# A long convolution by real transforms with a gated output: second stage with 128 moving columns, columns put right in the last table

## The chip, the cores and the metric

The kernel runs on one core of a Trainium2 chip. The metric is device time in microseconds, as the median of several runs. PE is the matrix engine (its weight loads are listed as PEld), DVE the vector engine, ACT the scalar engine, POOL the general engine, and SP the engine whose queue issues all DMA here. Matmuls write to PSUM, which DVE and ACT read and POOL doesn't.

## The reference

For x of shape [8, 6400, 128] and h of shape [6400, 128] (sequence, channel), the reference makes a causal convolution along the sequence, per channel, and then a gated mix of the channels, all in float32:

```python
Xf = np.fft.rfft(x, n=2*S, axis=1); Hf = np.fft.rfft(h, n=2*S, axis=0)
y = np.fft.irfft(Xf * Hf[None], n=2*S, axis=1)[:, :S]        # _attn_ref
for k in range(5):                                            # _moe_ref, on y
    gate_pre += conv_w[k] * y_padded[:, k:k + S]              # 4 zeros ahead
gate = 1 / (1 + np.exp(-gate_pre))
out = (gate * (y @ w_val)) @ w_out
```

## The kernel before, in words

**The transform.** The sequence is split as 6400 = N1 x N2 = 100 x 64, and the convolution is done by four stages of small matmuls with cosine and sine tables instead of an FFT. One frequency index is k1 (100 values, in two halves of HR = 50), the other k2 (64 values).

- *First stage* (`Forward`): a load brings XG = 4 channel pairs as XR = 114 rows (two channels, 50 rows each, the first padded to 64). POOL forms the difference and DVE or POOL the sum of mirrored halves (`sums`), and 16 matmuls, which the chip runs as 32 instructions since each float32 matmul is two, multiply them with the table r1 (`half`). ACT (and DVE in the opening) copies PSUM to `gh` for h or `gy` for a batch.
- *Second stage* (`s2_mm`, L271): for each block kb of SB = 4 values of k1 within a half (13 blocks, the last with 2), each value has its own table in m2. 128 rows are contracted to 64; output goes to the lower or the upper 64 PSUM partitions. Each matmul moves 64 columns: half of the channels. Four matmuls per value and component (two halves p of k1 times two channel halves k) go to the output half (p + k) % 2, so that the other half of the channels has the k1 halves exchanged.
- *Product* (`Product`, L302): with the spectrum of h, which was made in the same layout by `Spectrum`. DVE multiplies PSUM with the first component into `gy` (`mul_u`) and with the second into one of three tiles `w_t` (`mul_t`); POOL adds and subtracts (`add`). The spectrum of h is kept in DRAM (`hd`) and loaded again, block by block, for each later batch (`h_load`).
- *Third stage* (`s3_quads`): contracts the 64 values of k2, four 64 x 64 matmuls abreast, 128 columns each; ACT and DVE copy to `dt`.
- *Last stage* (`Chunk.s4`, L371): for each of the 64 positions n2, four matmuls with 100 columns of the table m4 (`m4v`, L345) give y, in 13 chunks of five positions (the head chunk: four).

**The gate.** Per chunk ACT copies y and makes some of the five taps straight from PSUM, DVE makes others, POOL adds one (`copies`, `taps`); then come PE's projection, ACT's sigmoid, DVE's product, PE's output matmul, and a copy and store.

**Order.** All instructions keep program order on their engines, written out by hand.

- *The opening*: the first stage for h, then for batch 0. The load ring has the three `x_sb` tiles and twelve more that lie in the not yet loaded m4 table.
- *The head*: the second stage for h (13 `Spectrum`) and batch 0 (13 `Product`) in turn. DVE decodes the 64-bit weights between products (`weights`). Each spectrum block is stored to `hd`.
- Then, per batch b, *stage A*: 16 groups, each with the third stage of batch b and the first of batch b + 1, the m2 and h loads for what follows, and a step of the `trail`, the late chunks of the batch before (`Gates.trail`); in batch 0 also 13 loads of m4. And *stage B*: 13 steps, each with the last stage of a chunk of batch b and the second stage and product of block s + 1 of batch b + 1; project, output and store of earlier chunks follow two to four steps behind. Chunks at DEFER = 40 or later (40, 45, 50, 55) only copy y in B; their taps, projection, gate, output and store, and those of the head chunk, are the trail of the next A. The last batch has no trail: it finishes in order.
- SP issues loads and stores in program order: in B, per step, an m load (after the block that used its tile), a store, and an h load (after the second DVE product, L632). Rings: m2 has M2B = 4 tiles, h has HB = 3, `w_t` has WB = 3.
- PSUM: two pools of two bank pairs in the opening and the head; afterwards one of them makes way for four single banks, which the third and last stage, projection and output share.

Of the kernel before, what the change touches and what calls it, by code (L numbers as in the profile page):

```python
# [10 lines left out]
F32 = mybir.dt.float32  # L11
# [21 lines left out]
NCH = len(CHUNKS)  # L33
OUT_ORDER = CHUNKS[1:] + [HEAD]
LATE = 35
DEFER = 40
M2B = 4
WB = 3
HB = 3
XB = 3  # L40


def _out_range(ch):
# [8 lines left out]
def _constants():  # L52
    k1 = np.arange(N1, dtype=np.float64)
    n1 = np.arange(N1, dtype=np.float64)
    k2 = np.arange(N2, dtype=np.float64)
    n2 = np.arange(N2, dtype=np.float64)
    half = np.arange(2 * HP) % HP
    own = half < HR
    tau = 2.0 * np.pi
    a = tau * np.outer(half + 0.5, k1 + 0.25) / N1  # L60
    r1 = np.stack([np.cos(a) + np.sin(a), np.cos(a) - np.sin(a)], axis=1) * own[:, None, None]
    al = tau * (
        (k1[None, :, None] + 0.25) * n2[:, None, None] / N
        + np.outer(n2, k2)[:, None, :] / N2
        - (k1[None, :, None] + 0.25) / (2 * N1)
    )
    co, si = np.cos(al) / 2, np.sin(al) / 2
    m2 = np.zeros((2, N2, N1, 2 * N2))
    m2[0, :, :, :N2] = co - si
    m2[0, :, :, N2:] = -si - co  # L70
    m2[1, :, :, :N2] = co + si
    m2[1, :, :, N2:] = co - si
    m2 = m2.reshape(2 * N2, 2, HR, 2 * N2).transpose(0, 2, 1, 3)
    b = tau * np.outer(k2, n2) / N2
    r3 = np.zeros((N2, 2, N2, 2))
    r3[:, 0, :, 0] = np.cos(b)
    r3[:, 1, :, 0] = -np.sin(b)
    r3[:, 0, :, 1] = -np.sin(b)
    r3[:, 1, :, 1] = -np.cos(b)
    r3 = np.concatenate([r3, r3], axis=0)  # L80
    t = N2 * n1[None, :] + n2[:, None]
    kk = half + HR * (np.arange(2 * HP) // HP)
    g = tau * (kk[:, None, None] + 0.25) * t[None] / N
    m4 = np.concatenate([np.cos(g), np.sin(g[:, :1])], axis=1) / N * own[:, None, None]
    f = lambda v: np.ascontiguousarray(v.astype(np.float32))
    return f(r1.reshape(2 * HP, -1)), f(m2), f(r3.reshape(2 * HP, -1)), f(m4.reshape(2 * HP, -1))

# [22 lines left out]
def longconv_moe(ctx: ExitStack, tc: tile.TileContext, x, h, r1, m2, r3, m4, w64, out):  # L110
# [11 lines left out]
    dt = cp.tile([128, N2 * 2 * C], F32, name="dt")  # L122
    dv = dt.rearrange("p (n c d) -> p n c d", c=2, d=C)
    gh = dt[:, : N1 * C].rearrange("p (d k t) -> p d k t", k=N1, t=2)
    m4_sb = cp.tile([128, N2 + 1, N1], F32, name="m4_sb")
    r1_sb = cp.tile([128, 2, N1], F32, name="r1_sb")
    r3_sb = cp.tile([128, 2, 2 * N2], F32, name="r3_sb")
    w_sb = cp.tile([C, NW], F32, name="w_sb")
# [7 lines left out]
    w_t = [cp.tile([128, 2 * SB * C], F32, name=f"w_{i}") for i in range(WB)]  # L136
# [73 lines left out]
    class Forward:  # L210


        def __init__(self, src, dst, xs=x_sb, o=0):
            self.src, self.dst, self.n, self.s, self.i, self.o = src, dst, 0, 0, 0, o
            self.xs = xs[o % len(xs) :] + xs[: o % len(xs)]

        def load(self, n=1):
            for _ in range(n):
                if self.n < NS:
                    nc.sync.dma_start(self.xs[self.n % len(self.xs)][:XR], self.src[self.n, :XR])  # L220
                    self.n += 1

        def sums(self, e):
            j = self.s
            if j >= NS:
                return
            self.s += 1
            x, sd = self.xs[j % len(self.xs)][:XR], sd_sb[(j + self.o) % 3][:XR]
            nc.gpsimd.tensor_tensor(out=sd[:, 1], in0=x[:, 0], in1=x[:, 1], op=ALU.subtract)
            e.tensor_tensor(out=sd[:, 0], in0=x[:, 0], in1=x[:, 1], op=ADD)  # L230
            self.load()
# [22 lines left out]
    def count(kb):  # L254
        return min(SB, HR - kb * SB)

    def m2_load(kb):
        if kb < NKB:
            n = count(kb)
            nc.sync.dma_start(m2_sb[kb % M2B][:, :n], m2[:, kb * SB : kb * SB + n])  # L260

    def h_load(kb):
        if kb < NKB:
# [4 lines left out]
        n = count(kb)  # L268
        return t[:, : 2 * n * C].rearrange("p (c d k t) -> p c d k t", c=2, k=n, t=2)

    def s2_mm(src, kb):  # L271
        pt = pair()
        n = count(kb)
        v = pt[:, :, : n * C].rearrange("p c (d k t) -> p c d k t", k=n, t=2)
        for s in range(n):
            for c in range(2):
                for p, k in ((0, 0), (1, 0), (1, 1), (0, 1)):
                    o = (p + k) % 2
                    nc.tensor.matmul(
                        v[o * N2 : (o + 1) * N2, c, k * C // 4 : (k + 1) * C // 4, s, :],  # L280
                        lhsT=m2_sb[kb % M2B][:, s, p, c * N2 : (c + 1) * N2],
                        rhs=src[:, k * C // 4 : (k + 1) * C // 4, p * HR + kb * SB + s, :],
                        start=True,
                        stop=True,
                    )
        return v

    hx = h_sb + [dt[:, N1 * C + i * 2 * SB * C : N1 * C + (i + 1) * 2 * SB * C] for i in range(3)]

    class Spectrum:  # L290
        def __init__(self, kb):
            self.kb, self.v = kb, s2_mm(gh, kb)
            self.h = hx[kb % len(hx)]

        def copy(self):
# [4 lines left out]
            nc.sync.dma_start(hd[self.kb, :, :n], self.h[:, :n])  # L300

    class Product:  # L302
        def __init__(self, kb, h=None):
            self.kb, self.v = kb, s2_mm(gy, kb)
            self.t = laid(w_t[kb % WB], kb)
            self.u = gy.rearrange("p d (c k) t -> p c d k t", c=2)[:, :, :, kb * SB : kb * SB + count(kb)]
            self.h = laid(h if h is not None else h_sb[kb % HB], kb)

        def both(self, c):
            h = self.h[:, c : c + 1]  # L310
# [31 lines left out]
            for k in range(2)  # L342
        ]

    def m4v(n, c):  # L345
        if c and n:
            return m4_sb[:, N2 - n, :][:, ::-1]
        return m4_sb[:, N2 if c else n, :]

    def cells(x, n):  # L350

# [10 lines left out]
    class Chunk:  # L362
# [8 lines left out]
        def s4(self):  # L371
            a, n = self.ch
            pt = single()
            for q in range(n):
                for c in range(2):
                    for k in range(2):
                        o = slice(k * HP, (k + 1) * HP)
                        nc.tensor.matmul(
                            pt[o, q * N1 : (q + 1) * N1],
                            lhsT=dv[:, a + q, c, o],  # L380
                            rhs=m4v(a + q, c),
                            start=c == 0,
                            stop=c == 1,
                        )
            self.p = pt[:, : n * N1].rearrange("p (n t) -> p n t", n=n)
# [85 lines left out]
        def store(self):  # L471
# [5 lines left out]

    wgen = weights()
    xh = x_sb + [
        m4_sb.rearrange("p n t -> p (n t)")[:, i * 2 * XG * N2 : (i + 1) * 2 * XG * N2].rearrange(  # L480
            "p (a d n) -> p a d n", a=2, n=N2
        )
        for i in range(12)
    ]
    fh, fx = Forward(h, gh, xh), Forward(x[0], gy, xh, NS)
    fh.load()
# [5 lines left out]
    for g, (f, i) in enumerate(order):  # L492
        e = f.half()
        if g + 2 < 2 * NS:
            order[g + 2][0].sums(nc.vector)
        if g + len(xh) >= NS:
            fx.load()
        e[0](act)
        e[1](act if g % 2 else dve)
    next(wgen)  # L500
    for kb in range(M2B):
        m2_load(kb)
    nc.sync.dma_start(r3_sb, r3)
    sp, pr = {0: Spectrum(0)}, {}
    for kb in range(-1, NKB + 1):
        if 0 <= kb < NKB:
            pr[kb] = Product(kb, sp[kb].h)
            m2_load(kb + M2B)
        if kb + 2 < NKB:
            sp[kb + 2] = Spectrum(kb + 2)  # L510
        if kb + 1 < NKB:
            sp[kb + 1].copy()
            sp[kb + 1].store()
        if 0 <= kb < NKB:
            pr[kb].mul_u()
# [8 lines left out]
    class Gates:  # L524
# [5 lines left out]
        def trail(self):  # L530

            h, late = self.cs[0], [c for c in self.cs if c.late]
            steps = collections.defaultdict(list)
            for m, c in enumerate(late):
                t = 2 * m + m // 2
                steps[t + 4].append(c.store)
                steps[t + 3].append(c.output)
                steps[t + 2] += [c.project, c.sigm, c.gate]
                steps[t].append(lambda c=c: c.taps(range(2)))
                steps[t + 1].append(lambda c=c: c.taps(range(2, 4)))  # L540
            n = max(steps) + 1
# [27 lines left out]
    for b in range(B):  # L569
# [8 lines left out]
        for g in range(NS):  # L578
# [107 lines left out]
```

## Time and profile before

| | us |
|---|---|
| median of 3 runs (lowest to highest) | 1040.47 (1040.33 to 1044.34) |
| the profiled execution's own time | 1044.37 |
| its span, first to last instruction | 1042.5 |
| PE busy in the span | 966.9 |
| DVE, POOL, ACT busy | 687.5, 552.1, 479.9 |

The span is the one core's. Every engine's instructions are recorded on one helper line (L97), so groups are told apart by their tiles: `pt` is PSUM, `r_sb` the tables r1 and r3, `m` the second stage's table, `m_sb` the last table, `h`, `w` and `dt` the spectrum, the second product, and the big tile that holds gh in the opening and head and the third stage's result later. A row of the order of time gives start, duration, engine, line, operation, tiles, shape and count, and in brackets the idle time ahead of it with what ended it. A matmul's duration contains the way through the array; the pace is read from start to start.

### The profile page before, as it was taken

The numbers are of one execution on the slowest core, as the hardware profiler recorded it, in microseconds if no ns is written. First come the engines' busy times: TensorE is split into PE (matmuls) and PEld (weight loads), VectorE is DVE, ScalarE is ACT, GpSimd is POOL, SyncE is SP. The second block draws the span as 40 slices with busy tenths as digits, with TensorE's granted clock in tenths as the row PEclk, the third lists the DMA queues.
The fourth block names the chain that finished last, engine by engine and source line by source line (L and its number), as shares of the span: only waits on it lengthen the run. The fifth ranks groups of instructions, "written<-read, shape, count | busy, mean of one in ns | idle before, by whom it ended". The sixth has DMA issues, their size and how long they took to land.

```text
span 1042.5 us, 54128 instructions
## 1 busy us (share of the span) xinstructions
PE 966.9 (93%) x24960; PEld 809.8 (78%) x24960; DVE 687.5 (66%) x932; ACT 479.9 (46%) x923; POOL 552.1 (53%) x558
## 2 busy tenths in 40 slices
PE   7997777999989998899989999999989999999987
PEld 6897767878787877888788878878788878877753
DVE  3447711897549772896559772996459772996476
ACT  3431133454534455355534455345534465344465
POOL 4534732577427862577437852677427852671032
PEclk9999899999999999999999999999999999999999
DMA  3566465674548554674558554774558554761012
GB/s 140 179 190 200 166 189 178 205 211 135 179 148 235 154 166 144 208 208 141 163 182 232 144 167 132 229 199 142 165 158 235 145 167 135 244 184 43 31 41 88
DMA packets 93409, 171.99 MB, mean 165 GB/s; under 512 B 41952, under 2 KB 50016, under 8 KB 93184
## 3 DMA queue, kind: packets, MB, share of 16 engines
q1 hardware_dynamic: 93184, 168.55, 53.4%
q8 instruction: 196, 3.21, 1.3%
q14 instruction: 29, 0.24, 0.1%
HBM read 135.75 MB, written 32.77 MB: 162 GB/s over the span
## 4 chain that ended last, share of the span: by engine, by line
PE 84%; issue 5%; DMA 4%; DVE 3%; SPq 1%; POOL 1%; ACT 0%; POOLq 0%; DVEq 0%
PE pt L97 84%; DMA x<-xl 1%; DVE gl L97 1%; DMA m_sb<-hl 1%; SPq L97 1%; DMA m_sb<-xl 1%; DVE dt L97 1%; POOL gl L97 1%; POOL dt L97 0%; DVE gy L97 0%; DMA x<-hl 0%; ACT dt L97 0%; DVE w L97 0%; POOLq L682 0%; POOL sd L97 0%
## 5 line engine op out<-in xcount | busy, mean ns | idle before, releaser
L97 POOL TENSOR_TENSOR gy<-gy,w 128x512 f32<-128x512 f32 (+1 forms) x206 | 253.3, 1253 | 85.2 <-DVE w L97 84.5
L97 PEld LDWEIGHTS pt<-r_sb,gy 64*64 64x64 f32 (+1 forms) x8192 | 236.0, 131 | 69.8 <-issue 51.3
L97 PE MATMUL pt<-r_sb,gy 64*50 64x128 f32 (+1 forms) x8192 | 266.6, 275 | 19.2 <-issue 13.0
L97 POOL TENSOR_TENSOR sd<-x 114x256 f32<-114x256 f32 x232 | 189.3, 839 | 162.6 <-issue 102.3
L97 ACT COPY dt<-pt 128x512 f32<-128x512 f32 (+3 forms) x270 | 157.1, 585 | 210.4 <-PE pt L97 205.8
L97 PEld LDWEIGHTS pt<-gy,m 128*64 128x64 f32 x6400 | 204.4, 136 | 40.5 <-issue 22.0
L97 PE MATMUL pt<-gy,m 128*64 128x64 f32 x6400 | 209.2, 221 | 14.8 <-issue 9.3
L97 PEld LDWEIGHTS pt<-m_sb,dt 128*64 128x64 f32 x4096 | 188.7, 137 | 43.6 <-issue 29.1
L97 PE MATMUL pt<-m_sb,dt 128*64 128x100 f32 x4096 | 196.5, 249 | 3.6 <-DVE dt L97 2.4
L97 DVE COPY dt<-pt 128x512 f32<-128x512 f32 (+1 forms) x136 | 92.7, 682 | 149.2 <-PE pt L97 148.2
L97 PE MATMUL pt<-r_sb,sd 50*64 50x100 f32 x4608 | 162.9, 278 | 24.2 <-issue 16.9
L97 PEld LDWEIGHTS pt<-r_sb,sd 50*64 50x64 f32 x4608 | 140.8, 154 | 37.9 <-issue 25.0
L97 DVE TENSOR_TENSOR gy<-pt,h 128x1024 f32<-128x1024 f32 (+1 forms) x98 | 115.2, 1175 | 43.3 <-PE pt L97 43.3
L97 DVE SCALAR_TENSOR_TENSOR dt<-pt,w_sb,dt 128x500 f32<-128x500 f32 (+7 forms) x216 | 132.9, 632 | 14.1 <-POOL dt L97 5.5
L97 ACT COPY gy<-pt 128x400 f32<-128x400 f32 x248 | 110.7, 497 | 60.4 <-PE pt L97 51.0
L97 DVE SCALAR_TENSOR_TENSOR gl<-yl,w_sb,gl 128x500 f32<-128x500 f32 (+1 forms) x119 | 105.5, 892 | 40.9 <-ACT gl L97 38.9
L97 ACT ACTIVATE dt<-pt,w_sb 128x500 f32<-128x500 f32 (+1 forms) x64 | 40.1, 627 | 167.3 <-PE pt L97 161.7
L97 PE MATMUL pt<-dt,w_sb 128*64 128x500 f32 (+2 forms) x480 | 114.8, 555 | 1.9 <-ACT p L97 1.0
L97 DVE TENSOR_TENSOR w<-pt,h 128x1024 f32<-128x1024 f32 (+1 forms) x98 | 114.9, 1172 | 0.0
L97 POOL TENSOR_TENSOR dt<-dt,p 128x500 f32<-128x500 f32 (+1 forms) x64 | 66.5, 1039 | 82.5 <-DVE dt L97 66.5
L97 ACT COPY yl<-pt 128x500 f32<-128x500 f32 (+1 forms) x96 | 54.5, 568 | 66.6 <-PE pt L97 66.6
L97 DVE TENSOR_TENSOR gl<-pt,gl 128x500 f32<-128x500 f32 (+1 forms) x48 | 31.7, 661 | 54.2 <-ACT gl L97 35.5
(34 smaller groups left out, 539.4 us busy)
## 6 DMA issues: line engine op xcount, KB each, us to landing
m<-m SPq DMA_DIRECT2D x96, 512.0 KB
h<-hd SPq DMA_DIRECT2D x84, 512.0 KB
x<-xl SPq DMA_DIRECT2D x116, 228.0 KB
out<-dt SPq DMA_DIRECT2D x56, 250.0 KB
out<-yl SPq DMA_DIRECT2D x40, 250.0 KB
m_sb<-m SPq DMA_DIRECT2D x13, 250.0 KB
hd<-h SPq DMA_DIRECT2D x6, 512.0 KB
hd<-dt SPq DMA_DIRECT2D x6, 512.0 KB
```

The costliest lines, as they stand in the source:

```text
L97: return self._tc.keep_in_program_order(call(*args, **kwargs))
```

## The change

The second stage drops the split of the channels: one matmul per value, component and half p of k1 moves all 128 columns, and half p always goes to output half p. For one half of the channels the two k1 halves are thereby exchanged against the layout of before. What that changes in the third and last stage goes into tables: r3 has its own lower and upper rows (k2 + 1/2 in the upper ones), and the last table now has, for each position, three blocks of 50 columns: those of even n1, those of odd n1, and the odd ones with the sign turned (MW = 150 columns instead of 100). The last stage reads two of the three blocks, the first and second for the one half of the channels and the first and third for the other, and writes them to every other place of PSUM, so that the result has its old order.

The second product is written over the spectrum tile instead of `w_t`, which is gone (in the head, where the spectrum still has to be stored, it goes to three tiles `t_head` within the m4 table). The rings change: h has 4 tiles, m2 has 3, and 6 in the head (three of them in the m4 table). The loads of the first stage bring all 128 rows instead of 114, the opening's ring has 8 tiles instead of 15. DEFER becomes 35, so the chunk at 35 joins the trail, whose steps are placed anew.

```diff
-XR = HP + HR
+MW = 3 * HR
-DEFER = 40
-M2B = 4
-WB = 3
-HB = 3
+DEFER = 35
+M2B = 3
+MH = 6
+HB = 4
 XB = 3
+XH = 8
...
-    b = tau * np.outer(k2, n2) / N2
-    r3 = np.zeros((N2, 2, N2, 2))
...
-    r3 = np.concatenate([r3, r3], axis=0)
-    t = N2 * n1[None, :] + n2[:, None]
-    kk = half + HR * (np.arange(2 * HP) // HP)
-    g = tau * (kk[:, None, None] + 0.25) * t[None] / N
-    m4 = np.concatenate([np.cos(g), np.sin(g[:, :1])], axis=1) / N * own[:, None, None]
+    r3 = []
+    for p in range(2):
+        b = tau * np.outer(k2 + p / 2, n2) / N2
+        c, d = np.cos(b), np.sin(b)
+        g = 1 - 2 * p
+        r3.append(np.stack([np.stack([c, -g * d], -1), np.stack([-d, -g * c], -1)], 1))
+    r3 = np.concatenate(r3, axis=0)
+    t = N2 * n1[None, :] + np.arange(N2 + 1)[:, None]
+    sign = np.where(np.arange(2 * HP)[:, None] < HP, 1.0, 1 - 2 * (n1 % 2))
+    m4 = np.cos(tau * (half[:, None, None] + 0.25) * t[None] / N) / N * own[:, None, None] * sign[:, None]
+    m4 = np.concatenate([m4[:, :, ::2], m4[:, :, 1::2], -m4[:, :, 1::2]], axis=2)
...
-                    nc.sync.dma_start(self.xs[self.n % len(self.xs)][:XR], self.src[self.n, :XR])
+                    nc.sync.dma_start(self.xs[self.n % len(self.xs)], self.src[self.n])
...
-            x, sd = self.xs[j % len(self.xs)][:XR], sd_sb[(j + self.o) % 3][:XR]
+            x, sd = self.xs[j % len(self.xs)], sd_sb[(j + self.o) % 3]
...
+    m4_flat = m4_sb.rearrange("p n t -> p (n t)")
+    m2_head = m2_sb + [
+        m4_flat[:, i * 2 * SB * C : (i + 1) * 2 * SB * C].rearrange("p (s a c) -> p s a c", a=2, c=C)
+        for i in range(M2B, MH)
+    ]
...
-                for p, k in ((0, 0), (1, 0), (1, 1), (0, 1)):
-                    o = (p + k) % 2
+                for p in range(2):
                     nc.tensor.matmul(
-                        v[o * N2 : (o + 1) * N2, c, k * C // 4 : (k + 1) * C // 4, s, :],
-                        lhsT=m2_sb[kb % M2B][:, s, p, c * N2 : (c + 1) * N2],
-                        rhs=src[:, k * C // 4 : (k + 1) * C // 4, p * HR + kb * SB + s, :],
+                        v[p * N2 : (p + 1) * N2, c, :, s, :],
+                        lhsT=ms[kb % len(ms)][:, s, p, c * N2 : (c + 1) * N2],
+                        rhs=src[:, :, p * HR + kb * SB + s, :],
...
+    t_head = [m4_flat[:, i * 2 * SB * C : (i + 1) * 2 * SB * C] for i in range(MH, MH + 3)]
...
-        def __init__(self, kb, h=None):
-            self.kb, self.v = kb, s2_mm(gy, kb)
-            self.t = laid(w_t[kb % WB], kb)
+        def __init__(self, kb, h=None, t=None, ms=m2_sb):
+            self.kb, self.v = kb, s2_mm(gy, kb, ms)
+            h = h if h is not None else h_sb[kb % HB]
...
-            self.h = laid(h if h is not None else h_sb[kb % HB], kb)
+            self.h, self.t = laid(h, kb), laid(t if t is not None else h, kb)
...
-    def m4v(n, c):
-        if c and n:
-            return m4_sb[:, N2 - n, :][:, ::-1]
-        return m4_sb[:, N2 if c else n, :]
+    def m4v(n, c, k):
+        v = m4_sb[:, N2 - n if c else n, :].rearrange("p (b m) -> p b m", m=HR)
+        if c:
+            return v[:, 1::-1, ::-1] if not k else v[:, ::-2, ::-1]
+        return v[:, 0:2, :] if not k else v[:, ::2, :]
...
-                            pt[o, q * N1 : (q + 1) * N1],
+                            pt[o, q * N1 : (q + 1) * N1].rearrange("p (m b) -> p b m", b=2),
                             lhsT=dv[:, a + q, c, o],
-                            rhs=m4v(a + q, c),
+                            rhs=m4v(a + q, c, k),
...
-        if g + len(xh) >= NS:
+        if NS - len(xh) <= g < NS:
             fx.load()
...
-    for kb in range(M2B):
-        m2_load(kb)
+    for kb in range(MH):
+        m2_load(kb, m2_head)
...
-            pr[kb] = Product(kb, sp[kb].h)
-            m2_load(kb + M2B)
+            pr[kb] = Product(kb, sp[kb].h, t_head[kb % 3], m2_head)
+            m2_load(kb + MH, m2_head)
...
-            for m, c in enumerate(late):
-                t = 2 * m + m // 2
-                steps[t + 4].append(c.store)
-                steps[t + 3].append(c.output)
-                steps[t + 2] += [c.project, c.sigm, c.gate]
-                steps[t].append(lambda c=c: c.taps(range(2)))
-                steps[t + 1].append(lambda c=c: c.taps(range(2, 4)))
-            n = max(steps) + 1
-            steps[n - 2] += [h.project, h.sigm, h.gate]
-            steps[n - 1].append(h.output)
-            steps[n].append(h.store)
+            for m, c in enumerate(late + [h]):
+                t = 2 * m + 2
+                if c is not h:
+                    steps[t - 2].append(lambda c=c: c.taps(range(2)))
+                    steps[t - 1].append(lambda c=c: c.taps(range(2, 4)))
+                steps[t] += [c.project, c.sigm, c.gate]
+                steps[t + 2].append(c.output)
+                steps[t + 3].append(c.store)
+            n = max(steps)
```

More of the change, by code (lines that the diff above doesn't have):

```diff
@@ L73, in _constants @@
     m2 = m2.reshape(2 * N2, 2, HR, 2 * N2).transpose(0, 2, 1, 3)
-    b = tau * np.outer(k2, n2) / N2
-    r3 = np.zeros((N2, 2, N2, 2))
[L76 to L79, printed above, removed]
-    r3 = np.concatenate([r3, r3], axis=0)
-    t = N2 * n1[None, :] + n2[:, None]
-    kk = half + HR * (np.arange(2 * HP) // HP)
-    g = tau * (kk[:, None, None] + 0.25) * t[None] / N
-    m4 = np.concatenate([np.cos(g), np.sin(g[:, :1])], axis=1) / N * own[:, None, None]
+    r3 = []
[9 more added lines that the diff above has]
+    m4 = np.concatenate([m4[:, :, ::2], m4[:, :, 1::2], -m4[:, :, 1::2]], axis=2)
     f = lambda v: np.ascontiguousarray(v.astype(np.float32))
@@ L124, in longconv_moe @@
     gh = dt[:, : N1 * C].rearrange("p (d k t) -> p d k t", k=N1, t=2)
-    m4_sb = cp.tile([128, N2 + 1, N1], F32, name="m4_sb")
+    m4_sb = cp.tile([128, N2 + 1, MW], F32, name="m4_sb")
     r1_sb = cp.tile([128, 2, N1], F32, name="r1_sb")
@@ L135, in longconv_moe @@
     sd_sb = [cp.tile([128, 2, XG, N2], F32, name=f"sd_{i}") for i in range(3)]
-    w_t = [cp.tile([128, 2 * SB * C], F32, name=f"w_{i}") for i in range(WB)]
     p_t = [cp.tile([128, CH, N1], F32, name=f"p_{i}") for i in range(2)]
@@ L255, in count, with m2_load @@
         return min(SB, HR - kb * SB)
-    def m2_load(kb):
+    m4_flat = m4_sb.rearrange("p n t -> p (n t)")
[3 more added lines that the diff above has]
+    ]
+    def m2_load(kb, ms=m2_sb):
         if kb < NKB:
             n = count(kb)
-            nc.sync.dma_start(m2_sb[kb % M2B][:, :n], m2[:, kb * SB : kb * SB + n])
+            nc.sync.dma_start(ms[kb % len(ms)][:, :n], m2[:, kb * SB : kb * SB + n])
     def h_load(kb):
@@ L269, in laid, with s2_mm @@
         return t[:, : 2 * n * C].rearrange("p (c d k t) -> p c d k t", c=2, k=n, t=2)
-    def s2_mm(src, kb):
+    def s2_mm(src, kb, ms=m2_sb):
         pt = pair()
@@ L288, in longconv_moe @@
     hx = h_sb + [dt[:, N1 * C + i * 2 * SB * C : N1 * C + (i + 1) * 2 * SB * C] for i in range(3)]
+    t_head = [m4_flat[:, i * 2 * SB * C : (i + 1) * 2 * SB * C] for i in range(MH, MH + 3)]
     class Spectrum:
         def __init__(self, kb):
-            self.kb, self.v = kb, s2_mm(gh, kb)
+            self.kb, self.v = kb, s2_mm(gh, kb, m2_head)
             self.h = hx[kb % len(hx)]
@@ L479, in longconv_moe @@
     xh = x_sb + [
-        m4_sb.rearrange("p n t -> p (n t)")[:, i * 2 * XG * N2 : (i + 1) * 2 * XG * N2].rearrange(
+        m4_flat[:, i * 2 * XG * N2 : (i + 1) * 2 * XG * N2].rearrange(
             "p (a d n) -> p a d n", a=2, n=N2
         )
-        for i in range(12)
+        for i in range(XH - XB)
     ]
@@ L589, in longconv_moe @@
                 a = CH * g
-                nc.sync.dma_start(m4_sb[:, a : a + CH], m4.rearrange("k (n t) -> k n t", t=N1)[:, a : a + CH])
+                nc.sync.dma_start(m4_sb[:, a : a + CH], m4.rearrange("k (n t) -> k n t", t=MW)[:, a : a + CH])
             if nxt and g % 2 and g > 1:
```

## The prediction

> **What bounds the kernel now.** I read the page first (busy shares, chain, queues), then the busy time by stretch, then the order of time of PE, DVE and POOL inside one stage of each kind.
>
> ```profile
> PE 966.9 (93%) x24960; PEld 809.8 (78%) x24960; DVE 687.5 (66%) x932; ACT 479.9 (46%) x923; POOL 552.1 (53%) x558
> ...
> q8 instruction: 196, 3.21, 1.3%
> ...
> PE 84%; issue 5%; DMA 4%; DVE 3%; SPq 1%; POOL 1%; ACT 0%; POOLq 0%; DVEq 0%
> ```
>
> PE is the bound by the page: 93% busy, 84% of the chain. Two smaller items matter as much here: 5% "issue" (some 52 us in which PE waits for nothing that is shown) and 4% DMA. By stretches (us, then busy time of PE, PEld, DVE, ACT, POOL, then clock, DMA share, GB/s):
>
> ```profile
> 10.00:44.00 34.00, 33.04 (x689) 28.12 (x685) 14.15 (x33) 14.75 (x33) 20.50 (x22) 1.00 0.40 154
> 48.00:52.00 4.00, 3.47 (x63) 2.68 (x60) 1.05 (x3) 1.66 (x5) 1.53 (x2) 1.00 1.05 265
> ...
> 122.00:183.00 61.00, 45.83 (x1532) 43.33 (x1530) 12.01 (x17) 22.75 (x46) 23.40 (x33) 0.92 0.54 168
> 479.00:532.00 53.00, 50.90 (x1574) 41.81 (x1576) 28.26 (x38) 30.08 (x61) 26.09 (x32) 1.00 0.51 158
> 416.00:479.00 63.00, 60.13 (x1392) 51.51 (x1386) 53.31 (x71) 26.43 (x51) 42.55 (x39) 1.00 0.66 193
> 424.00:430.00 6.00, 4.01 (x120) 3.76 (x116) 6.00 (x11) 1.13 (x3) 3.79 (x4) 1.00 0.93 323
> ```
>
> So there are four kinds of stage. The **opening** (first stage of h and of batch 0) ends where the first second-stage matmul starts, at 60.48. The **head** (second stage of h and batch 0) follows to 122.98. Then come in turn **stage A** (third stage of one batch, first of the next; 479 to 532) and **stage B** (last stage of one batch, second of the next; 416 to 479). A and B are PE's, except that in B DVE is 6.00 of 6.00 busy from 424 to 430 while PE has 4.01.
>
> The opening is not PE's. A load there lets POOL and DVE form sum and difference, then 32 matmuls run:
>
> ```profile
> 4.58 0.42 DVE L97 TENSOR_TENSOR sd<-x 114x256 f32<-114x256 f32 x1 [4.58 <-DMA x<-hl]
> ...
> 10.03 0.94 POOL L97 TENSOR_TENSOR sd<-m_sb 114x256 f32<-114x256 f32 x1 [0.66 <-DMA m_sb<-hl]
> 11.03 1.32 PEld L97 LDWEIGHTS pt<-r_sb,sd 50*64 50x64 f32 x32 [0.29 <-POOL sd L97]
> ...
> 11.56 0.98 POOL L97 TENSOR_TENSOR sd<-m_sb 114x256 f32<-114x256 f32 x1 [0.58 <-DMA m_sb<-hl]
> ...
> 60.48 5.19 PE L97 MATMUL pt<-dt,m 128*64 128x64 f32 x128
> ```
>
> POOL starts a load's work every 11.56 - 10.03 = 1.53 us and then waits for the DMA. Yet the DMA engines are only 0.40 busy: 114 rows a load use about six of the sixteen (6/16 = 0.375). When the 128-row loads of m come between (48 to 52) the share is 1.05.
>
> In the head DVE sets the pace, until PE is stopped from outside:
>
> ```profile
> 67.67 1.22 DVE L97 TENSOR_TENSOR gy<-pt,h 128x1024 f32<-128x1024 f32 x1 [7.44 <-PE pt L97]
> ...
> 71.55 1.21 DVE L97 TENSOR_TENSOR gy<-pt,h 128x1024 f32<-128x1024 f32 x1
> ...
> 75.38 1.21 DVE L97 TENSOR_TENSOR gy<-pt,h 128x1024 f32<-128x1024 f32 x1
> ...
> 121.11 1.87 DVE L97 TENSOR_TENSOR gy<-gy,w 128x256 f32<-128x256 f32 x2
> ```
>
> ```profile
> 85.21 1.75 PE L97 MATMUL pt<-dt,m 128*64 128x64 f32 x53 [2.24 <-issue]
> 86.79 2.06 PE L97 MATMUL pt<-gy,m 128*64 128x64 f32 x64
> 88.67 0.51 PE L97 MATMUL pt<-dt,m 128*64 128x64 f32 x10
> 89.76 1.75 PE L97 MATMUL pt<-dt,m 128*64 128x64 f32 x53 [0.58 <-issue]
> ```
>
> Between two stops lie 53 + 64 + 10 = 127 matmuls and as many weight loads. The page's 49,920 PE instructions over its 196 instruction packets give 255 a packet: PE waits for its next packet of instructions.
>
> **The change, part by part.**
>
> *Second stage, 128 columns (s2_mm, L271).* A steady stretch of B:
>
> ```profile
> 447.22 2.09 PE L97 MATMUL pt<-gy,m 128*64 128x64 f32 x64
> 449.12 1.03 PE L97 MATMUL pt<-dt,w_sb 128*64 128x500 f32 x4
> 449.96 1.91 PE L97 MATMUL pt<-m_sb,dt 128*64 128x100 f32 x40
> 451.68 1.03 PE L97 MATMUL pt<-dt,w_sb 128*64 128x500 f32 x4
> 452.51 2.06 PE L97 MATMUL pt<-gy,m 128*64 128x64 f32 x64
> ```
>
> From start to start, 64 instructions of 64 columns take 1.90 us (29.7 ns each) and 40 of 100 columns 1.72 us (43.0 each). The line through both is 0.37 ns a column plus 6; at 128 columns it gives 53.4 ns. The matmuls that already move 128 columns, in stage A:
>
> ```profile
> 480.74 0.87 PE L97 MATMUL pt<-r_sb,sd 50*64 50x100 f32 x32
> 481.43 1.93 PE L97 MATMUL pt<-r_sb,gy 64*64 64x128 f32 x64
> 483.17 0.87 PE L97 MATMUL pt<-r_sb,sd 50*64 50x100 f32 x32
> ```
>
> take 1.74 us for 64, four abreast in quarters of the array, so 54.4 ns for two abreast. A block of a kb becomes 32 instructions, 32 x 54 = 1.73 instead of 1.87 to 1.90 us: 0.15 saved, 12.5 blocks a batch. Bounds: 0, if what 64 columns pay over the line's slope belongs to the scattered pairs that they read and write (their number stays); 0.17 by the line. A loss is excluded: columns and pairs are the same, and half the weight loads go. The first three blocks of each B save nothing, since DVE is the bound there (424:430). So 9.5 x 0.15 x 7 = 10 us, bounds 0 and 15. The cover behind it is thin:
>
> ```profile
> 447.20 1.22 DVE L97 TENSOR_TENSOR gy<-pt,h 128x1024 f32<-128x1024 f32 x1
> 448.45 2.29 DVE L97 SCALAR_TENSOR_TENSOR dt<-pt,w_sb,dt 128x500 f32<-128x500 f32 x3
> 450.65 1.22 DVE L97 TENSOR_TENSOR w<-pt,h 128x1024 f32<-128x1024 f32 x1
> 451.79 0.67 DVE L97 TENSOR_TENSOR dt<-pt,dt 128x500 f32<-128x500 f32 x1
> 452.37 1.22 DVE L97 TENSOR_TENSOR gy<-pt,h 128x1024 f32<-128x1024 f32 x1
> ```
>
> DVE's step is 5.17 us and all but some 0.1 of it work; PE's is 452.51 - 447.22 = 5.29 and becomes 5.14. DVE is next, with nearly nothing to spare, so I take 9 rather than 10. [...]
>
> *Head.* Without stops DVE's 3.83 us a kb (75.38 - 71.55) covers PE's two blocks (2 x 1.88 = 3.76, then 3.46). From the first product to the end that is 11 x 3.83 + 2.3 + 1.3 + 1.9 = 47.6 us; the trace has 67.67 to 122.98, 55.3, so stops cost 7.7. After the change a packet of instructions lasts two kb, 7.7 us, instead of 3.8, twice as long to fetch the next, and PE has 0.4 a kb in hand. Before the first product stand three blocks: 3 x 0.15 saved. I take 8 us; bounds 0.5 (stops stay) and 9.
>
> *Loads of 128 rows (XR goes, L217), 8 buffers ahead instead of 15.* 14% more bytes, but in the shape of the loads that drove the share to 1.05. Bounds for the opening's pace: 1.53 x 128/114 = 1.72 if the shape changes nothing; else whatever comes next, POOL at 0.96 + 0.06 = 1.02 or PE at 1.31 (the 32 weight loads of one load, at 11.03; the same 32 matmuls take 481.43 - 480.74 = 0.69 in stage A). Whether PE stays at half its later pace, no row can tell: I take the middle, 1.17. Then 32 x 1.17 = 37.4 us from the start at 4.6, and the head starts at about 43 instead of 60.48: 17.5 us saved, bounds 13 (PE) and 22 (POOL), and 6 lost if the shape changes nothing. Eight loads ahead cover 8 x 1.17 = 9.4 us; the first landed 4.58 us after the start, so the shorter ring is hidden; if it weren't, the loads would fall back towards 1.53. [...]
>
> *Product in place, M2B 3, HB 4 (L302, L257).* The same DVE instructions write their second product over the spectrum tile. The tile comes free when POOL's two adds are done, not when DVE has read it, and the h load that waits for it stands on SP ahead of the next m load and the next store.
>
> ```profile
> L97 POOL TENSOR_TENSOR gy<-gy,w 128x512 f32<-128x512 f32 x192 | 243.6, 1291 | 85.2 <-DVE w L97 84.5
> ```
>
> So that load starts 2 x 1.29 = 2.6 us later. It is wanted four steps on, 4 x 5.14 = 20 us, and the m load behind it two to three steps on; both stay hidden by PE's work, at nothing. With the cover gone it would be up to 2.6 us a step.
>
> *Last stage (s4, m4v).* The same 4096 matmuls of 100 columns, now read as two runs of 50 and written to every other place. No row has this form. Nearest is the second stage, which writes pairs eight apart and pays 29.7 against 0.37 x 64 = 23.7 + 6; I take 0. Bounds: 0 and, if a write to every other place takes double, 176 us (4096 x 43.0 ns). A gain has no source.
>
> *Table half as long again, DEFER 35, trail respaced.* The table's loads
>
> ```profile
> m_sb<-m SPq DMA_DIRECT2D x13, 250.0 KB
> ```
>
> grow to 375 KB (1.6 MB more in all) and fall in 122:183, DMA share 0.54: hidden, +-5 us, since PE's stops there may grow. The chunk at 35 moves its projection and output (0.84 us each) from B to A, both PE's: no gain. Its taps and gate leave DVE in B (2.2 + 0.6 us) for A, where DVE is idle 53 - 28.3 = 24.7 us, and its store leaves SP in B (DMA share 0.66) for A (0.51).
>
> **Sum.** 1042.5 - 17.5 - 8 - 9 = 1008 span, plus the 1.9 around it in the profiled execution (1044.37). The median of the runs, 1040.47, lies 3.9 below that execution, so on its scale 1040.5 - 34.5 = **1006 us**.
>
> **Rivals.**
> - *Columns don't matter in the second stage.* The excess belongs to the scattered pairs: the 9 us go, opening and head stay. 1015. For it: the 6 ns over the slope are read off two forms, and only one of them is scattered. Against: 128 contiguous columns (54.4) pay about the same over the slope.
> - *The wider loads are no faster*, so the change doesn't do what it may: 1.72 a load, +6 instead of -17.5. 1029.5. For it: SP's issue could be the limit. Against: 1.05 share at 48:52.
> - *Packets of instructions go on stopping PE, and DVE takes over in B*: 7.5 back in the head and 4 in the batches. 1017.
> - *The last stage's writes to every other place cost double*: 1006 + 176 = 1182, slower. It decides from 34.5/176 = 20% more a matmul. Against: the second stage writes in larger strides and is near the line.
>
> **Chances.** Forecast 0.58, columns 0.15, loads 0.10, stops and DVE 0.09, writes 0.06, else 0.02. The forecast's own range is 995 (opening at POOL's pace, batches at 15) to 1014. The 8-in-10 range runs from 993 to the loads' case, 1030. About 0.5%, 5 us, is what a measurement of this kernel can tell from no change: faster by more 0.88, within 0.05, slower 0.07.
>
> **What would show it.** Opening: POOL's differences every 1.0 to 1.3 us, the first second-stage matmul at 38 to 48 us, DMA share well over 0.40. Head: DVE every 3.83 us without issue stops. B: 32-instruction blocks in 1.7 us, s4's 40 still 1.72, a step of 5.15. Wrong it would be with POOL at 1.5 or more, blocks at 1.88, s4 over 2 us, or SP waits on POOL followed by PE waits on m.

## The result

The changed kernel takes 1004.91 us (median of 4 runs, 1003.10 to 1006.82) beside 1040.40 for the kernel before: a ratio of 0.965, 95% interval 0.962 to 0.969. Faster, as forecast, and within 1.1 us of the forecast 1006. The gain itself is less sure than that: in a later set of runs (experiment 0) it was 28.5 us, where the forecast had 34.5 and the first set 35.5.

The page of the changed kernel, the same three lines as before:

```profile
PE 940.5 (94%) x21360; PEld 793.5 (79%) x21360; DVE 702.8 (70%) x939; ACT 475.5 (47%) x916; POOL 544.5 (54%) x551
...
q8 instruction: 167, 2.74, 1.1%
...
PE 90%; issue 5%; DVE 3%; POOL 1%; ACT 1%; DMA 0%; POOLq 0%; DVEq 0%; ACTq 0%
```

3600 matmul instructions and 29 instruction packets are gone, and DMA is gone from the chain. The changed kernel's busy time by stretch (opening, head, first stage A; then four pieces of the opening):

```profile
4.00:46.00 42.00, 35.38 (x1034) 32.57 (x1036) 24.79 (x47) 21.16 (x48) 25.94 (x32) 0.88 0.84 274
46.00:97.00 51.00, 45.87 (x796) 45.61 (x792) 45.27 (x51) 13.24 (x15) 30.37 (x24) 0.97 0.65 214
97.00:154.60 57.60, 45.23 (x1537) 42.45 (x1537) 12.33 (x17) 22.70 (x46) 23.78 (x33) 0.94 0.62 213
19.10:22.50 3.40, 3.40 (x92) 3.40 (x88) 2.29 (x5) 1.78 (x4) 2.23 (x3) 0.50 0.67 217
13.00:18.00 5.00, 4.00 (x148) 3.31 (x138) 4.78 (x9) 3.43 (x8) 4.47 (x5) 1.00 0.81 243
...
4.50:12.20 7.70, 7.70 (x173) 7.41 (x176) 3.38 (x8) 2.95 (x7) 5.41 (x7) 1.00 0.98 352
32.80:39.40 6.60, 6.52 (x157) 6.52 (x160) 2.60 (x7) 2.98 (x7) 3.42 (x5) 0.50 0.88 271
```

In the opening the DMA share went from 0.40 to 0.84 and the rate from 154 to 274 GB/s; in the changed kernel the first six loads of the second stage's table fall in it too, in its last 12 us.

To compare kernels I cut each profiled execution at the same instructions: the opening ends with the first second-stage matmul, the head with the first third-stage matmul, each stage A with the first matmul of the last stage, each stage B with the next third-stage matmul. All in us; "stops" is the time in which both PE and its weight loads were idle for over 0.25 us and nothing that is shown ended it, summed over the same trace (how a stop is told from another short wait moves these sums by up to some 2 us).

| kernel | opening | head | first A | seven B | A of batches 1 to 6 | last A and last stage | stops |
|---|---|---|---|---|---|---|---|
| before | 60.5 | 61.2 | 61.7 | 434.6 | 326.1 | 98.5 | 36.1 |
| changed | 45.5 | 51.6 | 57.5 | 422.5 | 323.8 | 104.2 | 23.0 |
| changed, run again | 46.4 | 52.7 | 57.5 | 422.5 | 318.4 | 102.9 | 21.3 |
| 64 columns again | 46.5 | 56.4 | 60.2 | 427.7 | 322.3 | 102.9 | 26.4 |
| 114 rows again | 60.9 | 53.7 | 60.0 | 422.4 | 326.6 | 102.9 | 21.0 |
| before, 128 rows | 46.7 | 63.3 | 57.5 | 433.2 | 315.3 | 98.6 | 35.3 |
| DEFER 40 again | 46.5 | 53.0 | 57.6 | 434.1 | 320.7 | 100.1 | 29.6 |
| before, 128 rows, DEFER 35 | 47.3 | 64.4 | 59.4 | 423.3 | 317.0 | 103.0 | 28.1 |
| ring of 4 in the head | 46.0 | 51.6 | 56.5 | 422.5 | 317.0 | 103.0 | 13.1 |

So the 37.5 us of the two spans are: opening -15.0, head -9.6, first A -4.2, the B stages -12.1, the other A stages -2.3, the last A and last stage +5.7. The small ones are within what traces of one kernel differ by: the two of the changed kernel lie 5.4 us apart in A of batches 1 to 6, and the trace before is of the slowest of its four executions.

In the head DVE now runs through, with the pace that the prediction read:

```profile
51.36 1.22 DVE L98 TENSOR_TENSOR gy<-pt,h 128x1024 f32<-128x1024 f32 x1 [5.35 <-PE pt L98]
...
55.23 1.21 DVE L98 TENSOR_TENSOR gy<-pt,h 128x1024 f32<-128x1024 f32 x1
...
59.07 1.21 DVE L98 TENSOR_TENSOR gy<-pt,h 128x1024 f32<-128x1024 f32 x1
...
96.50 1.87 DVE L98 TENSOR_TENSOR gy<-gy,m_sb 128x256 f32<-128x256 f32 x2
```

55.23 to 59.07 is 3.84 us a kb, and 51.36 to 98.37 is 47.0 us, where the prediction had 47.6. In stage B a step of PE, and DVE beside it:

```profile
412.02 2.02 PE L98 MATMUL pt<-gy,m 128*64 128x128 f32 x32
413.87 1.01 PE L98 MATMUL pt<-dt,w_sb 128*64 128x500 f32 x4
414.71 1.89 PE L98 MATMUL pt<-m_sb,dt 128*64 128x100 f32 x40
416.43 1.01 PE L98 MATMUL pt<-dt,w_sb 128*64 128x500 f32 x4
417.26 2.03 PE L98 MATMUL pt<-gy,m 128*64 128x128 f32 x32
```

The block of 32 instructions takes 413.87 - 412.02 = 1.85 us, not 1.73, and the step 5.24, not 5.14. The last stage's 40 still take 1.72: its new reads and writes cost nothing. So the width itself saved almost nothing in stage B, and yet the B stages are shorter by 12.1 us, where the forecast had 9. That is what the experiments had to settle.

### The profile page after: what moved, and what is told of

It is laid out like the page before. It is cut to its first block, busy times and chain, and to the rows that moved or that the text cites. A ratio compares the mean times of both kernels' runs of the same rounds, so it can differ in the third digit from the quotient of the medians.

```text
span 1005.0 us, 46982 instructions
## 1 busy us (share of the span) xinstructions
PE 940.5 (94%) x21360; PEld 793.5 (79%) x21360; DVE 702.8 (70%) x939; ACT 475.5 (47%) x916; POOL 544.5 (54%) x551
## 4 chain that ended last, share of the span: by engine, by line
PE 90%; issue 5%; DVE 3%; POOL 1%; ACT 1%; DMA 0%; POOLq 0%; DVEq 0%; ACTq 0%
PE pt L98 90%; DVE gl L98 1%; DVE dt L98 1%; POOL gl L98 1%; ACT dt L98 1%; DVE gy L98 0%; POOL dt L98 0%; DMA x<-hl 0%; DVE sd L98 0%; DVE m_sb L98 0%; POOLq L688 0%; ACT gl L98 0%; ACT yl L98 0%; ACT gy L98 0%; DVEq L98 0%
## 5 line engine op out<-in xcount | busy, mean ns | idle before, releaser
L98 PE MATMUL pt<-r_sb,gy 64*64 64x128 f32 (+1 forms) x8192 | 267.3, 273 | 20.3 <-issue 11.5
L98 POOL TENSOR_TENSOR sd<-x 128x256 f32<-128x256 f32 x236 | 197.4, 860 | 154.2 <-issue 124.2
L98 POOL TENSOR_TENSOR gy<-gy,h 128x512 f32<-128x512 f32 (+1 forms) x182 | 221.6, 1241 | 63.6 <-DVE h L98 27.7
L98 PEld LDWEIGHTS pt<-m_sb,dt 128*64 128x64 f32 x4096 | 191.5, 137 | 35.3 <-issue 22.7
L98 PEld LDWEIGHTS pt<-gy,m 128*64 128x64 f32 x3008 | 179.1, 135 | 43.8 <-issue 23.6
L98 PE MATMUL pt<-gy,m 128*64 128x128 f32 x3008 | 193.3, 278 | 17.5 <-issue 12.0
L98 PE MATMUL pt<-r_sb,sd 50*64 50x100 f32 x4608 | 143.2, 258 | 17.2 <-issue 11.2
L98 DVE SCALAR_TENSOR_TENSOR gl<-yl,w_sb,gl 128x500 f32<-128x500 f32 x147 | 130.6, 892 | 24.6 <-ACT gl L98 22.1
L98 PEld LDWEIGHTS pt<-r_sb,sd 50*64 50x64 f32 x4608 | 128.9, 142 | 22.2 <-issue 14.5
L98 DVE TENSOR_TENSOR h<-pt,h 128x1024 f32<-128x1024 f32 (+1 forms) x91 | 107.3, 1179 | 2.3
L98 ACT COPY yl<-pt 128x500 f32<-128x500 f32 (+1 forms) x96 | 54.5, 568 | 83.9 <-PE pt L98 83.9
L98 DVE TENSOR_TENSOR gl<-pt,gl 128x500 f32<-128x500 f32 (+1 forms) x48 | 31.7, 661 | 54.5 <-PE pt L98 50.8
```

What stands on the lines that cost most here:

```text
L98: return self._tc.keep_in_program_order(call(*args, **kwargs))
```

## The experiments

**0. The changed kernel again**, beside the second kernel of experiment 4, that of 5 and the first of 8, with nothing edited.

> The changed kernel itself, to have it beside the others on one chip. 1003 to 1007 us if the time depends on the kernel alone; the kernel before took 1040 beside its first runs and 1033 beside the first experiments, so a ratio between 0.965 and 0.972.

1003.89 us (1001.13 to 1005.80) beside 1032.36 for the kernel before, ratio 0.973 (0.970 to 0.975). The kernel before differs more from set to set than the changed one (1040.40 and 1032.36 against 1004.91 and 1003.89), so each experiment is compared with its own set.

**1. The second stage split again.** Only the width goes back; layout, tables and rings stay.

```diff
-                for p in range(2):
+                for p, k in ((0, 0), (1, 0), (0, 1), (1, 1)):
                     nc.tensor.matmul(
-                        v[p * N2 : (p + 1) * N2, c, :, s, :],
+                        v[p * N2 : (p + 1) * N2, c, k * C // 4 : (k + 1) * C // 4, s, :],
...
-                        rhs=src[:, :, p * HR + kb * SB + s, :],
+                        rhs=src[:, k * C // 4 : (k + 1) * C // 4, p * HR + kb * SB + s, :],
```

> The changed kernel with its second stage split again into two matmuls of 64 columns, one for each half of the channels, in the changed layout; all else as changed. Theory P (the gain of head and batches is fewer packets of instructions, not the width): a block of 64 instructions takes 1.87 against 1.84 us, packets go from 167 back to about 195, PE's issue waits from about 23 to 35 us, the head is 5 to 8 us longer and the batches together 7 to 10: 1016 to 1023 us. Rival L (the gain comes from the other edits: the head's ring of six, the 16-engine loads, DEFER 35): 1005 to 1009 us, with issue waits near 23.

1017.27 us (1011.73 to 1020.77), ratio to before 0.982 (0.976 to 0.989), within theory P's time. The trace has 195 packets. The head is 56.4, 3.7 to 4.9 us longer than in the two traces of the changed kernel and not 5 to 8, and in it DVE waits again where PE had stopped:

```profile
77.08 1.23 DVE L98 TENSOR_TENSOR gy<-pt,dt 128x1024 f32<-128x1024 f32 x1 [0.35 <-PE pt L98]
...
86.66 1.23 DVE L98 TENSOR_TENSOR gy<-pt,h 128x1024 f32<-128x1024 f32 x1 [1.79 <-PE pt L98]
```

But the seven B are 427.7, of which 3.5 us are stops: without these some 424, against 422.5. Theory P is right in kind for the head, too high in size, and wrong for the B stages, where the gain didn't go away with the width. Rival L has that part.

**2. Loads of 114 rows again**, with everything else as changed.

```diff
-                    nc.sync.dma_start(self.xs[self.n % len(self.xs)], self.src[self.n])
+                    nc.sync.dma_start(self.xs[self.n % len(self.xs)][:XR], self.src[self.n, :XR])
```

> The changed kernel with the first stage's loads and sums of 114 rows as before; all else as changed. If the width of the loads made the opening shorter: POOL's differences every 1.53 us again, head from about 59 instead of 45.5 us, 1017 to 1020 us. If the 114-row loads also lie behind PE's instruction stops in stage A (they crowd six DMA engines), issue waits after the head rise by 8 us or more and the time is 1025 us or more. If the shorter ring or PE's half clock set the opening, the head starts at 45 to 48 us still.

1026.33 us (1024.29 to 1028.99). POOL is back at its old pace, and the head starts at 60.91:

```profile
21.45 0.97 POOL L99 TENSOR_TENSOR sd<-x 114x256 f32<-114x256 f32 x1 [0.65 <-DMA x<-hl]
22.98 0.94 POOL L99 TENSOR_TENSOR sd<-m_sb 114x256 f32<-114x256 f32 x1 [0.55 <-DMA m_sb<-hl]
```

The opening is 60.9 instead of 45.5 to 46.4, and the loads' width is all that was edited. The time came out in the second theory's region (1025 or more), but its sign, more stops after the head, is weak: 8.8 us in the later A stages of this trace against 6.5 and 2.1 in the two of the changed kernel. I leave that open.

**3. The kernel before with 128-row loads alone.**

> The kernel before with the 128-row loads as its only edit. If the loads make the opening: head from about 45 us instead of 60.5, 1024 to 1028 us. If the wider loads also take away stops of PE in stage A: 1015 to 1020 us. If they are no faster: 1040 to 1046 us.

1019.40 us (1016.41 to 1025.11) beside 1032.99, ratio 0.986 (0.980 to 0.991): 13.6 us, the size of the opening's gain (60.5 to 46.7). The head stays long, 63.3, with 9.9 us of stops, and the B stages stay at 433.2. The time lies in the region of the second theory, and the A stages of batches 1 to 6 are 10.8 us shorter than in the trace before; as that trace is the slowest execution of its kernel, whether the wider loads also take stops out of stage A stays open here too.

**4. What a second-stage matmul pays for.** Two kernels that change only addresses, in the batches: one reads 128 neighbouring columns of another table, one writes to 128 neighbouring places. Their products are therefore not formed from the right data.

```diff
-                        rhs=src[:, :, p * HR + kb * SB + s, :],
+                        rhs=r3_sb[:, 0].rearrange("p (d t) -> p d t", t=2) if ms is m2_sb else src[:, :, p * HR + kb * SB + s, :],
```

> The changed kernel, but in the batches (not in the head) the second stage's matmuls read 128 neighbouring columns of the table r3 instead of the scattered pairs of gy; so the products of batches 1 to 7 are not formed from the data. Theory R (the 7% that a block takes over the pace of the last stage are its scattered reads): 32 instructions in 1.71 us instead of 1.84. Theory W (its scattered writes) or F (a fixed cost of a matmul of this form): 1.84 still.

```diff
-                        v[p * N2 : (p + 1) * N2, c, :, s, :],
+                        pt[p * N2 : (p + 1) * N2, c, s * C : (s + 1) * C].rearrange("q (d t) -> q d t", t=2)
```

> The changed kernel, but in the batches the second stage writes its 128 results to neighbouring places of PSUM instead of scattered pairs, while the products still read the old order; so the products of batches 1 to 7 are permuted. Theory R (reads): 32 instructions in 1.84 us still. Theory W (writes): 1.71.

Steps of the two, the one with neighbouring reads first:

```profile
410.70 1.97 PE L98 MATMUL pt<-r_sb,m 128*64 128x128 f32 x32
412.50 1.01 PE L98 MATMUL pt<-dt,w_sb 128*64 128x500 f32 x4
...
415.89 1.92 PE L98 MATMUL pt<-r_sb,m 128*64 128x128 f32 x32
417.63 1.01 PE L98 MATMUL pt<-dt,w_sb 128*64 128x500 f32 x4
```

```profile
401.42 2.07 PE L98 MATMUL pt<-gy,m 128*64 128x128 f32 x32
403.29 1.04 PE L98 MATMUL pt<-dt,w_sb 128*64 128x500 f32 x4
```

With neighbouring reads a block takes 1.74 us (417.63 - 415.89), the first one 1.80; two matmuls run abreast, and from one's start to that of the next but one the median is 109 ns, 54.5 for each, against 115, 57.5 for each, in the changed kernel. With neighbouring writes a block takes 1.87 (403.29 - 401.42) and the median is 115 ns as in the changed kernel. So theory R holds: what the second stage pays over matmuls with neighbouring columns is the reading of pairs. With 64 columns (experiment 1) a matmul of pairs takes 29.5 ns, half of 57.5 and 0.8 more: the price goes by the column, so that fewer and wider matmuls pay it all the same. The seven B are 416.4 with neighbouring reads, 0.9 us each below 422.5, and unchanged (422.4) with neighbouring writes. The whole times are one run each, 1000.13 and 1000.11 us, too few to tell the two apart.

**5. The moved chunk.** DEFER back to 40, everything else as changed.

> The changed kernel with DEFER 40: the chunk at 35 is finished in stage B as before; all else as changed. Theory as in the prediction (the move is PE's work from one PE-bound stage to another): within 2 us of the changed kernel. Rival (DVE's step of 5.05 us is so near PE's 5.24 that the moved taps give PE air in stage B): 1 to 2 us more a batch, 7 to 14 us in all, seen as longer steps and PE stops on DVE in stage B.

1013.77 us (1011.15 to 1013.96) beside 1003.89 for the changed kernel in the same set: 9.9 us. One stage B of each, by its first last-stage matmul and the first third-stage matmul after it; the kernel with DEFER 40, then the changed one:

```profile
388.00 1.60 PE L98 MATMUL pt<-m_sb,dt 128*64 128x100 f32 x31
...
449.99 1.11 PE L98 MATMUL pt<-r_sb,gy 64*64 64x128 f32 x32
```

```profile
268.15 1.68 PE L98 MATMUL pt<-m_sb,dt 128*64 128x100 f32 x31
...
328.52 1.22 PE L98 MATMUL pt<-r_sb,gy 64*64 64x128 f32 x36
```

61.99 against 60.37: the chunk's projection and output, 1.68 us of PE. The prediction took it at nothing because it would come back in stage A, and it doesn't: A of batches 1 to 6 is 320.7 with DEFER 40 and 318.4 with 35 in this set. The rival's reason, DVE giving PE air, isn't it either: it named longer steps, and the steps are the same; a chunk's PE work is missing. Only the last A, which has no first stage beside it, pays, with 46.1 us for 43.2.

**6. The two parts alone.** The kernel before with 128-row loads, DEFER 35 and the new trail, and with its old second stage, tables, rings and product.

> The kernel before with two edits alone: loads of 128 rows, and DEFER 35 with the new places of the trail; second stage, tables, products and rings as before. Theory (opening from the loads, stage B shorter by the moved chunk, stage A little longer because the chunk fills what stops left): stage B 60.4 instead of 62.0 us, opening 46 us, head 61 to 63 us with its stops, 1010 to 1016 us. Rival (stage B is shorter by the wide second stage together with the chunk): stage B 61.5 us or more, 1018 us or above.

1013.23 us (1005.17 to 1016.21) beside 1028.54, ratio 0.982 (0.974 to 0.990), as the theory has it. One stage B:

```profile
396.88 1.67 PE L97 MATMUL pt<-m_sb,dt 128*64 128x100 f32 x31
...
457.54 1.22 PE L97 MATMUL pt<-r_sb,gy 64*64 64x128 f32 x36
```

60.66 us with 64-column blocks, and the seven are 423.3: the B stages' gain needs nothing of the wide second stage. In the whole time the chunk's gain isn't clear in the old kernel: experiment 3, without the move, has the ratio 0.986, and the intervals overlap. Its trace and this one end within 0.2 us of each other; the 9.9 us of the seven B are given back in the other stages, 4.4 of them in the last A and last stage. What is missing against the changed kernel is the head, 64.4 us, where PE stops, and starts again slowly (62 matmuls over 3.13 us where they take 2.0 elsewhere; the granted clock is 0.50 from 86.2 to 89.6):

```profile
85.14 2.29 PE L97 MATMUL pt<-dt,m 128*64 128x64 f32 x54 [2.83 <-issue]
87.12 0.31 PE L97 MATMUL pt<-gy,m 128*64 128x64 f32 x1
87.22 0.31 PE L97 MATMUL pt<-dt,m 128*64 128x64 f32 x1
87.23 3.13 PE L97 MATMUL pt<-gy,m 128*64 128x64 f32 x62
```

**7. The head's ring.** MH from 6 to 4.

> The changed kernel with a ring of 4 instead of 6 tiles for m in the head. If the head got free of PE's stops by fewer packets of instructions (128 columns): head 52 to 53.5 us, DVE without idle time, 1004 us. If the longer ring (loads ahead of the head, so fewer DMAs beside the packets) did it: DVE idle again by 3 us or more in the head, which is then 55 us or longer, 1007 us or above.

1001.35 us (998.38 to 1003.51) beside 1028.54, ratio 0.972 (0.965 to 0.980). The head is 51.6 and DVE runs through without a wait from 51.85:

```profile
51.85 1.22 DVE L98 TENSOR_TENSOR gy<-pt,h 128x1024 f32<-128x1024 f32 x1 [5.36 <-PE pt L98]
...
96.96 1.87 DVE L98 TENSOR_TENSOR gy<-gy,m_sb 128x256 f32<-128x256 f32 x2
```

So with 128 columns the length of the ring doesn't matter. With 64 it may: experiment 1, with the ring of six, has 2.1 us of stops in the head, the kernels with the old second stage and its ring of four (experiments 3 and 6) have 9.9 and 9.5 with the same number of matmuls. Four tiles with 64 columns in the changed kernel were not run. Whether the shorter ring is better than the longer can't be told: the ratios to before are the same.

**8. Other layouts, to read more than pairs.** Three kernels keep the 128 columns and store gy and gh so that the second stage reads longer runs: all 128 channels side by side for each k1, or blocks of four or eight channels. The tile of the first:

```diff
-    gy = cp.tile([128, C // 2, N1, 2], F32, name="gy")
+    gyk = cp.tile([128, N1, C], F32, name="gy")
+    gy = gyk.rearrange("p k (d t) -> p d k t", t=2)
```

> The changed kernel with gy and gh laid out by k1 (128 channels side by side for each k1), so that the second stage reads 128 neighbouring columns and writes 128 neighbouring places; the spectrum and the products follow in that order. Theory R (scattered reads): 32 instructions in 1.70 instead of 1.84 us, 10 to 12 us in the batches, 990 to 995 us. Rival: the third stage's weights, now 512 bytes apart, and the first stage's copies, now in pieces of 8 bytes, cost as much or more: stage A longer by 2 us or more each, 1003 us or above.

> The changed kernel with gy and gh in blocks of four channels: the second stage reads runs of 4 instead of 2, the first stage's copies write whole blocks, the third stage's weights lie 16 bytes apart instead of 8. If the cost of scattered reads falls with the length of the runs and that of weights grows only with far wider steps: 32 instructions of the second stage in 1.77 us or less, stage A unchanged, 997 to 1003 us. If weights 16 bytes apart already cost more than 136 ns: stage A longer, 1005 us or above.

> The same in blocks of eight channels: runs of 8, weights 32 bytes apart. If it goes as hoped for the blocks of four: 32 instructions in 1.73 us or less, 996 to 1002 us. If the weights' price grows with their step: weight loads between 136 and 237 ns, stage A longer by 1 to 5 us, 1005 to 1035 us.

All three bring the pace to 54.5 ns and the seven B to 416.5, and none is faster than the changed kernel, by the ratio to before: 1037.56 us (ratio 1.006, 1.003 to 1.009), 1006.76 (0.977, 0.970 to 0.983) and 1009.45 (0.980, 0.973 to 0.987); the changed kernel has 0.965 and 0.973. The third stage takes gain back. Its weight loads, by form, in the changed kernel (run again), with all channels side by side, and in blocks of four (busy us, mean ns of one, idle time ahead):

```profile
L98 PEld LDWEIGHTS pt<-r_sb,gy 64*64 64x64 f32 x4096 | 172.2, 136 | 56.9 <-ACT gl L98 20.4 <-issue 13.6 <-DVE gl L98 5.5
```

```profile
L98 PEld LDWEIGHTS pt<-r_sb,gy 64*64 64x64 f32 x4096 | 237.5, 237 | 49.3 <-ACT gl L98 25.9 <-POOL gy L98 6.9 <-issue 5.6
```

```profile
L98 PEld LDWEIGHTS pt<-r_sb,gy 64*64 64x64 f32 x4096 | 202.2, 198 | 53.5 <-ACT gl L98 25.9 <-issue 14.4 <-POOL gy L98 6.9
```

136 ns with weights 8 bytes apart, 198 with 16, 237 with 512, and 202 with 32 in the blocks of eight; the loads of the second stage's table in the batches, whose weights are neighbours, take 135 to 137 ns in all four kernels. Stage A grows to 58.7 us with all channels side by side. With blocks of four it is 54.1 and with eight 54.5, where the changed kernel run again has 52.4 to 53.6; but its first trace has 53.0 to 55.5, so for these two the loss in stage A is less sure.

## Why the prediction was right, and where not

The time and the sign were right, two of the three terms were right in kind, and the third came out at its size by a mechanism that the prediction had priced at nothing.

- **Opening** (17.5 forecast, bounds 13 and 22; 15.0 measured). The mechanism holds: experiments 2 and 3 move the opening by 14 to 15 us with the loads' width alone. (A load of 128 rows has 12% more bytes than one of 114, not the 14% of the prediction; its sums use the right figure.) The size was off because PE, not the middle between PE and POOL, set the pace: from PE's first matmul at 3.9 us to 45.47 a load took 1.30 us, as in PE's bound of 1.31, and from 9.4 us on POOL waited for PE and not for DMA (the last rows below). The record of the granted clock shows 1.00 from 13 to 18, 0.50 from 19.1 to 22.5 and again from 32.7 to 39.5; in the slow pieces 32 matmuls take 1.33 us, in the fast one 0.87. Ahead of the record's first entry, at 12.2 us, the pace is the slow one as well (173 matmuls in 7.70 us), though the row reads 1.00; the 0.88 that the record gives for the opening's 42 us is thus too high. Some 5 us more are stops at the ends of packets (five of them, 0.28 to 2.12 us each), which the old opening didn't have.

  From PE's first matmul to the first slow piece no stop was longer than 1.51 us (the second row below, the changed kernel's PE in the opening) and none between the two longer than 0.80 (the third). What made the clock fall is not shown. The share of the DMA engines went from 0.40 with 114 rows a load to 0.84 with 128; what decides how many engines a load keeps busy is not shown either.

```profile
10.73 6.33 PE L98 MATMUL pt<-r_sb,sd 50*64 50x100 f32 x209
18.57 4.62 PE L98 MATMUL pt<-r_sb,sd 50*64 50x100 f32 x126 [1.51 <-issue]
...
32.88 9.28 PE L98 MATMUL pt<-r_sb,sd 50*64 50x100 f32 x252 [0.80 <-issue]
```

```profile
33.95 0.73 POOL L98 TENSOR_TENSOR sd<-x 128x256 f32<-128x256 f32 x1 [1.64 <-PE pt L98]
35.28 0.92 POOL L98 TENSOR_TENSOR sd<-x 128x256 f32<-128x256 f32 x1 [0.61 <-PE pt L98]
36.61 0.73 POOL L98 TENSOR_TENSOR sd<-m_sb 128x256 f32<-128x256 f32 x1 [0.42 <-PE pt L98]
```

- **Head** (8 forecast, bounds 0.5 and 9; 9.6 measured). Right by its own steps: DVE's floor of 47.6 us came as 47.0, and the stops of PE no longer reach DVE. That the 128 columns are enough for this is shown by experiment 7, and that the width counts by experiment 1, where 64 columns bring part of DVE's waits back (head 56.4). The other 7 to 8 us up to the 63 to 64 of experiments 3 and 6 are not separated; the ring together with the 64 columns is a rival that was not run. The measured gain passes the upper bound by what lies ahead of the first product: 5.9 us (51.36 - 45.47) instead of 7.2 (67.67 - 60.48), where the prediction took 0.45 off; the two first blocks of the old head still ran at the slow pace, 5.0 us instead of 3.8.
- **Second stage in the batches** (9 forecast). This step failed. A block takes 1.85 us where 1.73 was drawn from the line through two forms and from the third stage. The line took a cost that each column pays (57.5 - 54.5 = 3.0 ns in 128 columns of pairs) for one that each matmul pays. The prediction's own rows could have told: a line through its two forms with neighbouring columns, 43.0 ns at 100 and 54.4 at 128, gives 28.3 at 64, so that 64 columns of pairs paid 1.4 more; twice that on 54.4 is an estimate of 57.2. The rival "columns don't matter" was right on this term, and the bound of 0 that belonged to it held.
- **The moved chunk** (0 forecast). The other failed step, with the other sign. Its 1.68 us of PE left each B, 12 us in seven, and A of batches 1 to 6 didn't grow beyond what the traces differ by. Part of the reason is to be seen: stage A has air that stage B has not. In A of batches 1 to 6 stops take 13.3 us with DEFER 40 and 2.1 with 35 (experiment 5 and the changed kernel again), and 8.2 and 1.5 in the old kernel (experiments 3 and 6), so the chunk's work took the place of stops. But other traces with DEFER 35 have up to 8.8, and why the stops grow fewer when there is more work is not shown. That the trail's projections and outputs now share their steps may help as well; it wasn't tried alone.
- **Last A** (not in the sum). It has no first stage to fill, and the longer trail takes it from 41.4 to 46.1 us. The prediction priced the move for the seven batches and forgot this one.
- **Priced at nothing and right**: the last stage's writes to every other place (40 in 1.72 us before and after). Of the product in place, the later h loads, the larger table and the ring of 8 the trace shows no cost (DMA has 0% of the chain), but none of them was run alone.

Stage by stage the two traces differ by -15 - 9.6 - 4.2 - 12.1 - 2.3 + 5.7 = -37.5, against -34.5 forecast. That the failed term and the chunk, which was taken at nothing, were of about the same size is luck; the trace shows it only when B is cut from A. That the time came within 1.1 us is in part luck too, as the kernel before has taken 1028.5 to 1040.4 us from set to set.

## What to carry to other kernels

Look at the rows of a load before its bytes: 12% more bytes, in 128 rows instead of 114, took the share of the DMA engines that worked in the opening from 0.40 to 0.84 and were the largest single gain, 15.0 us of 37.5. When a sum agrees with the time, check it stage by stage all the same, and draw a line only through forms that are read and written alike: the two forms here differed in width and in pattern at once. And a program that issues tens of thousands of small matmuls (24,960 here, then 21,360) can stop between packets of them (2.83 us in the row of experiment 6): fewer, wider ones helped in the head here (51.6 and 52.7 us, and 56.4 with 64 columns), where no slope of the matmul itself shows it.

## What the runs showed of the hardware

- Reading moving columns in pairs costs a float32 matmul of 128 columns 57.5 instead of 54.5 ns (two abreast); runs of four already give the full pace. Writing pairs costs none of it (57.5 with neighbouring writes too), and writing every other place none that the last stage shows (40 matmuls in 1.72 us before and after).
- The third stage's weight loads took longer the farther their elements lay apart: 136 ns at 8 bytes, 198 at 16, 202 at 32, 237 at 512.
- The page of the changed kernel has 256 PE instructions to a packet (2 x 21,360 over 167), and most of PE's stops in the traces before and after lie 252 to 256 instructions apart, or a multiple of that; so PE seems to wait there for the next packet, up to 2.83 us in the rows of experiment 6.
- In the old opening the record of the clock shows 1.00 although 32 matmuls took about 1.3 us, twice their later time (0.69 in stage A): the record's entries are changes, 1.00 and 0.50 in turn, and its first is at 63.2 us, a change to 1.00. The pace is the better witness.
